# Two of eight weight slots of the first token pair in the seven-product form, with their operand sums early in that pair

## The chip, the cores and the metric

The kernel runs on one core of one Trainium2 chip. The metric is the device time of one execution in microseconds (us), as the median of several runs. The engines named below are TensorE (PE, with PEld for its weight loads), VectorE (DVE), ScalarE (ACT), GpSimd (POOL) and SyncE (SP), which issues most of the DMAs.

## What is computed

The reference is a chunked attention with eight memory tokens, followed by two feed-forward blocks, all in float32:

```python
x = attention(q, k, v, mem_k, mem_v)          # 3072 tokens x 512
h = x @ w_in                                  # 512 -> 2048, the "input product"
g = h * tanh(where(h > 20, h, log1p(exp(min(h, 20)))))
x = g @ w_out                                 # 2048 -> 512
xn = x / sqrt(mean(x * x) + 1e-6) * rms_g
gate, val = xn @ w_gate, xn @ w_val           # 512 -> 1536 each
out = (gate / (1 + exp(-gate)) * val) @ w_out2
```

The weights arrive as 64-bit floats and are converted on the chip. Each float32 operand is held as a rounded part (hi) and a rest (lo), and a product of two operands is three matmuls: hi by hi, hi by lo, lo by hi.

## The kernel before

The change lies in the input product. Its 3072 tokens are eight blocks of 384, taken as four pairs of blocks, and its 2048 output rows are eight weight slots i of 256 rows. The attention of the pair that comes next runs between the matmuls of the pair at hand, so the kernel goes through four stages: attention of pair 0, then the product of pair j beside the attention of pair j + 1.

There are two forms of the product. In the plain form, `unit(b, i)` multiplies slot i with one block b: two output halves, two halves of the 512 inputs, each a `product` of six matmuls (two 128-row pieces by three), so 24 matmuls, and 48 for both blocks of a pair. Its results leave PSUM by one ACT copy per output half (L691). In the seven-product form, `group1(j, i)` treats a slot and a pair of blocks as 2x2 block matrices and needs seven products of six matmuls, 42 in all. It wants sums of blocks as operands: on the weight side `finish(("i", i))` makes them out of a plain converted slot (four DVE additions of 512 and 256 columns, two on POOL, two splits into hi and lo), on the token side `sum_pieces` makes them out of the two blocks `xb` (four DVE operations, L615 to L618, and splits into tiles T). A split is an ACT copy (hi, L153) and a DVE subtraction (lo, L154). Its results leave PSUM by three ACT copies, four DVE operations and one on POOL.

Before the change, pair 0 is plain in all eight slots. Slots 0 to 2 of block 0 are done among the last steps of the attention of pair 0 (`heads`); the other 13 units run in the list `units`, at lines 1045 to 1052: block 1 with slots 0, 1, 2, then both blocks with 3, 4, 7, 5, 6. Pairs 1 to 3 are all in the seven-product form, with the slots in the order 7 to 0 for pair 1.

What stands between the matmuls is set by `slots`: its function `between` is called after each product of six matmuls, and does the next piece of attention, the next step of the weight conversion (`cv_upto`, as a line through a first and a last count), what stands in the table `more` for this count, and over the last seven counts the operand sums of the next pair (`tail_of`). A scheduler then orders each engine's instructions by its own simulation; each engine runs its own list in that order, and an instruction that waits holds up all behind it on its engine.

The tiles T come from a pool of eight buffers (`tp`); pair 0 uses four of them, one for each half of each block, made by `x_split`. The temporary sums and the results share the five buffers named g. In the rows below bk_82 to bk_85 are the PSUM banks of the products, bk_86 and bk_87 those of transposes, and bkp that of the attention's small matmuls (L457 for scores, L506 for values). L393, L436, L489 and L532 are transposes of k, q, the probabilities and the result; L470 and L471 are the maximum and the subtraction of it, L476 the exponential, L539 the copy of an attention result into xb, L202 to L216 the conversion of weights.

## Time and profile before

| what | value |
|---|---|
| median of three runs | 1168.31 us (1165.23 to 1170.05) |
| span of the profiled execution | 1167.0 us |
| PE busy | 1142.3 us, 98% of the span |
| DVE, ACT, POOL busy | 824.7 (71%), 628.7 (54%), 183.3 us (16%) |
| granted TensorE clock, mean | 0.994 |

The span runs from the first to the last instruction; of the profiled execution the page gives no time beside it, and the median of the runs lies 1.31 us above it. The 13 units of pair 0 that the change touches lie at about 66 to 144 us; the product of pair 1 follows. From 65 us on, PE's idle time before any instruction is rarely over 0.4 us. The clock is given as a share of 2.4 GHz.

### The profile page before, as it was taken

The page shows a single profiled execution, that of the slowest core. Times are in us where ns is not written, and L with a number is a line of the kernel's source. Part 1 is how long each engine was busy: PE and PEld are TensorE (multiplying, and loading weights), DVE is VectorE, ACT ScalarE, POOL GpSimd, SP SyncE. Part 2 cuts the span into 40 slices and gives each one's busy share as a digit, 9 for nine tenths or more (in the row PEclk, how much of TensorE's full clock was granted, in tenths as well). Part 3 has the DMA queues.
Part 4 walks back from the last instruction along what each step waited for, and adds up shares of the span by engine and source line. Part 5 has one row for each costly group of instructions (what it writes and reads, how often), then busy time and mean ns, then how long its engine had stood idle before and what let it go on. Part 6 is the DMA issues. An engine that isn't in the chain of part 4 may idle for free.

```text
span 1167.0 us, 22953 instructions
## 1 busy us (share of the span) xinstructions
PE 1142.3 (98%) x9052; PEld 1007.0 (86%) x9052; DVE 824.7 (71%) x1254; ACT 628.7 (54%) x1008; POOL 183.3 (16%) x165
## 2 busy tenths in 40 slices
PE   6899999999999999999999999999999999999998
PEld 4789999999999888888878778888888888999998
DVE  3555798844746876766786765967896857888883
ACT  4566666543555887667775543544454433444441
POOL 3011222310132321010011121110211111000000
PEclk9799999999999999999999999999999999999999
DMA  9889699899488764594599398999899879655421
GB/s 197 171 228 224 183 303 258 230 307 290 151 300 295 257 217 161 172 378 152 199 362 408 126 345 325 349 410 355 316 361 371 316 276 332 191 148 146 145 90 37
DMA packets 213276, 294.20 MB, mean 252 GB/s; under 512 B 104240, under 2 KB 160560, under 8 KB 204336
## 3 DMA queue, kind: packets, MB, share of 16 engines
q1 hardware_dynamic: 210864, 284.34, 73.6%
q0 software_dynamic: 2304, 8.39, 2.3%
q8 instruction: 71, 1.16, 0.4%
q14 instruction: 37, 0.30, 0.1%
HBM read 181.80 MB, written 110.89 MB: 251 GB/s over the span
## 4 chain that ended last, share of the span: by engine, by line
PE 83%; DVE 7%; DMA 5%; ACT 3%; issue 2%; SPq 0%; POOL 0%; ACTq 0%; DVEq 0%
PE bk L639 14%; PE bk L640 13%; PE bk L641 13%; PE bk L914 4%; PE bk L913 4%; PE bk L912 4%; PE bk L755 4%; PE bk L756 4%; PE bk L754 4%; PE bkp L639 2%; PE bkp L641 2%; PE bkp L640 2%; PE bkp L506 1%; PE bkp L457 1%; PE bkp L755 1%
## 5 line engine op out<-in xcount | busy, mean ns | idle before, releaser
L639 PE MATMUL bk<-T,w 128*128 128x384 f32 (+1 forms) x860 | 315.2, 370 | 0.7 <-ACT c L657 0.7
L640 PE MATMUL bk<-T,w 128*128 128x384 f32 (+1 forms) x860 | 311.3, 362 | 0.0
L641 PE MATMUL bk<-T,w 128*128 128x384 f32 (+1 forms) x860 | 308.3, 362 | 0.0
L639 PEld LDWEIGHTS bk<-T,w 128*128 128x128 f32 x860 | 162.3, 189 | 19.9 <-ACT c L657 1.0
L640 PEld LDWEIGHTS bk<-T,w 128*128 128x128 f32 x860 | 162.2, 189 | 16.5 <-DVE T L154 0.3
L641 PEld LDWEIGHTS bk<-T,w 128*128 128x128 f32 x860 | 161.8, 188 | 15.7
L913 PE MATMUL bk<-w,T 128*128 128x256 f32 x396 | 111.9, 283 | 0.0
L914 PE MATMUL bk<-w,T 128*128 128x256 f32 x396 | 111.9, 283 | 0.0
L912 PE MATMUL bk<-w,T 128*128 128x256 f32 x396 | 111.9, 283 | 0.0
L755 PE MATMUL bk<-T,w 128*128 128x512 f32 x276 | 107.5, 390 | 0.2 <-DVE T L154 0.2
L756 PE MATMUL bk<-T,w 128*128 128x512 f32 x276 | 107.1, 389 | 0.0
L754 PE MATMUL bk<-T,w 128*128 128x512 f32 x276 | 105.8, 389 | 0.0
L669 POOL TENSOR_TENSOR v<-c,v 128x512 f32<-128x512 f32 x36 | 54.7, 1519 | 289.2 <-DVE c L665 238.8
L665 DVE TENSOR_TENSOR c<-bk,c 128x512 f32<-128x512 f32 (+2 forms) x72 | 43.0, 597 | 51.2 <-PE bk L641 38.6
L912 PEld LDWEIGHTS bk<-w,T 128*128 128x128 f32 x396 | 76.0, 192 | 0.1
L913 PEld LDWEIGHTS bk<-w,T 128*128 128x128 f32 x396 | 76.0, 192 | 0.1
L914 PEld LDWEIGHTS bk<-w,T 128*128 128x128 f32 x396 | 76.0, 192 | 0.0
L649 ACT COPY c<-bk 128x512 f32<-128x512 f32 (+2 forms) x72 | 37.1, 516 | 69.6 <-POOL v L669 24.7
L154 DVE TENSOR_TENSOR T<-s,T 128x1024 fp32r<-128x1024 f32 (+1 forms) x50 | 63.1, 1269 | 14.3 <-ACT T L153 14.2
L782 ACT ACTIVATE s<-s 128x1024 f32<-128x1024 f32 x44 | 46.4, 1060 | 29.7 <-DMA s<-g_scratch 29.5
L755 PEld LDWEIGHTS bk<-T,w 128*128 128x128 f32 x276 | 51.8, 188 | 11.3 <-DVE T L154 0.6
L754 PEld LDWEIGHTS bk<-T,w 128*128 128x128 f32 x276 | 51.8, 188 | 10.8
(228 smaller groups left out, 2287.1 us busy)
## 6 DMA issues: line engine op xcount, KB each, us to landing
T<-nt_scratch SPq DMA_DIRECT2D x35, 1024.0 KB
g_scratch<-g SPq DMA_DIRECT2D x64, 384.0 KB
s<-g_scratch SPq DMA_DIRECT2D x46, 512.0 KB
h_scratch<-s SPq DMA_DIRECT2D x36, 512.0 KB
w<-wg SPq DMA_DIRECT2D x10, 1792.0 KB
wg<-w SPq DMA_DIRECT2D x30, 512.0 KB
raw<-in_moe_w_out_dram SPq DMA_DIRECT2D x28, 512.0 KB
nt_scratch<-T SPq DMA_DIRECT2D x14, 1024.0 KB
```

The lines of the kernel that those rows point to most:

```text
L154: keep((eng or nc.vector).tensor_tensor(lo, src, hi.bitcast(F32), op=ALU.subtract))
L639: nc.tensor.matmul(ps, whi, xh, start=first and kk == 0, stop=False, **more)
L640: nc.tensor.matmul(ps, whi, xl, start=False, stop=False, **more)
L641: nc.tensor.matmul(ps, wlo, xh, start=False, stop=kk == 1, **more)
L669: nc.gpsimd.tensor_tensor(c22, u3, z5, op=ALU.add)
L754: nc.tensor.matmul(ps, ahi, bhi, start=start, stop=False)
L755: nc.tensor.matmul(ps, ahi, blo, start=False, stop=False)
L756: nc.tensor.matmul(ps, alo, bhi, start=False, stop=stop)
L782: nc.scalar.activation(x, g, self.act)
L912: nc.tensor.matmul(ps, t[:, 0, f], w[:, 0], start=first and f == 0, stop=False, **more)
L913: nc.tensor.matmul(ps, t[:, 0, f], w[:, 1], start=False, stop=False, **more)
L914: nc.tensor.matmul(ps, t[:, 1, f], w[:, 0], start=False, stop=f == HG - 1, **more)
```

## The change

Slots 4 and 7 of pair 0 move to the seven-product form, and the order of the slots becomes: block 1 with 0, 1, 2; both blocks with 3; groups 4 and 7; both blocks with 5 and 6 ("the last two plain"). The token sums of pair 0 are made in the first five counts of the stage (`first_sums`), out of the blocks in place, into the four T buffers that pair 0 had left free (`T_FIRST` takes all eight at once); products 1, 2 and 3 use the T tiles that `x_split` made. `finish` of slots 4 and 7 stands three counts ahead of their groups; that of slot 4 was in the stage of pair 1 before. The weight conversion line is steeper (80 steps over 50 counts, where it was 73 over 52).

```diff
+    T_FIRST = [t_new() for _ in range(8)]
+    X_AT = {(0, 0): 4, (0, 1): 5, (1, 0): 6, (1, 1): 7}
+    P_AT = {6: 0, 5: 1, 4: 2, 7: 3}
     def x_split(b, half):
-        t = t_new()
+        t = T_FIRST[X_AT[b, half]]
...
-    units = [(1, i) for i in range(NHEAD)]
-    units += [(b, i) for i in (3, 4, 7, 5, 6) for b in range(2)]
-    at = {u: 4 * n + 4 for n, u in enumerate(units)}
+    units = [(1, i) for i in range(NHEAD)] + [(b, 3) for b in range(2)]
+    whole = (4, 7)
+    after = [(b, i) for i in (5, 6) for b in range(2)]
+
+    def first_sums():
+        b11, b21, b12, b22 = (xb[b][:, 2 * half:2 * half + 2, :] for b in range(2) for half in range(2))
+        early, rest = sum_pieces(0, b11, b21, b12, b22, lambda: T_FIRST[P_AT[first_p.pop(0)]],
+                                 lambda p: g_new(), None, ttab_x)
+        return [early[1]] + rest[0:3] + rest[4:5]
+
+    first_p = [6, 5, 4, 7]
     more = {}
-    finish_at(more, 7, at[1, 7] + 1)
-    bt = slots((att_list(1), 4 * len(units)), (0, 73), tail_of(1), calls(more), CV_I)
+    for n, call in enumerate(first_sums()):
+        then(more, n + 1, call)
+    for p, bh in ((1, (0, 0)), (2, (0, 1)), (3, (1, 1))):
+        ttab_x[0, p] = xtab[bh]
+    n_slots = 4 * len(units + after) + 7 * len(whole)
+    for n, i in enumerate(whole):
+        finish_at(more, i, 4 * len(units) + 7 * n - 3)
+    bt = slots((att_list(1), n_slots), (0, 80), tail_of(1), calls(more), CV_I)
     for b, i in units:
         run([unit(b, i)], bt)
+    for i in whole:
+        group1(0, i, bt)
+    for b, i in after:
+        run([unit(b, i)], bt)
...
-    for n, i in enumerate((6, 5, 4, 3)):
-        finish_at(more, i, 3 * n + 1)
+    for n, i in enumerate((6, 5, 3)):
+        finish_at(more, i, 4 * n + 1)
```

What this does to the order shows at three places. The first is ACT's list at the start of the pair, where the second block of the pair is finished and split. L406 and L407 copy transposed keys, L153 with w is the hi part of slot 2's second half, L153 with T that of block 1. Before:

```order
L407 COPY kw<-bk_86 128x4x32
L539 COPY xb<-bk_87 128x4x128
L153 CAST w<-ca 128x2x2x128
L153 CAST T<-xb 128x768 x2
L447 COPY qT<-bk_87 128x512
L406 COPY kw<-bk_86 128x4x3x56
L407 COPY kw<-bk_86 128x4x32
L202 ACTIVATE ca<-raw 128x512
L205 ACTIVATE lr<-raw 128x512
```

The same stretch of ACT's list after the change:

```order
L407 COPY kw<-bk_86 128x4x32
L202 ACTIVATE ca<-raw 128x512
L205 ACTIVATE lr<-raw 128x512
L539 COPY xb<-bk_87 128x4x128
L153 CAST w<-ca 128x2x2x128
L406 COPY kw<-bk_86 128x4x3x56
L407 COPY kw<-bk_86 128x4x32
L153 CAST T<-xb 128x768 x2
```

The two conversion steps L202 and L205 of the next weight half now stand ahead of the last copy into xb and of the slot's cast.

The second place is DVE's list at the same time, from the last parts of the block's split to the next maximum of the attention. Before:

```order
L410 COPY kw<-kw 128x16x8
L154 TENSOR_TENSOR w<-ca,w 128x2x2x128
L402 COPY kw<-bk_86 128x4x24
L154 TENSOR_TENSOR T<-xb,T 128x768 x2
L470 TENSOR_REDUCE mx<-bkp 128x8
```

The same stretch of DVE's list after the change:

```order
L210 SCALAR_TENSOR_TENSOR ca<-raw,ca 128x512
L615 TENSOR_TENSOR xb<-xb 128x768
L154 TENSOR_TENSOR w<-ca,w 128x2x2x128
L154 TENSOR_TENSOR T<-xb,T 128x768 x2
L616 TENSOR_TENSOR g<-xb 128x768
L618 TENSOR_TENSOR xb<-xb 128x768
L617 TENSOR_TENSOR g<-g,xb 128x768
L154 TENSOR_TENSOR T<-g,T 128x768
L154 TENSOR_TENSOR T<-xb,T 128x768
L154 TENSOR_TENSOR T<-g,T 128x768
L154 TENSOR_TENSOR T<-xb,T 128x768
L470 TENSOR_REDUCE mx<-bkp 128x8
```

A conversion step and the first sum now stand ahead of the lo part of slot 2's second half, and eight operations of 768 columns in all are new there.

The third place is PE's list at the end of the pair, from the last matmuls of the last unit to the first product of pair 1. The rows with bk_85 belong to the unit, those with bk_82 to pair 1. Before, the last transpose L532 of the attention of pair 1 stands 24 matmuls ahead of the unit's end, and the list ends with:

```order
L639 MATMUL bk_85<-T,w 128x384
L640 MATMUL bk_85<-T,w 128x384
L641 MATMUL bk_85<-T,w 128x384
L393 MATMUL bk_87<-ident,kn 128x128
L436 MATMUL bk_86<-ident,qn 128x128 x4
L393 MATMUL bk_87<-ident,kn 128x128 x3
L639 MATMUL bk_82<-T,w 128x384
```

The end of PE's list of pair 0 after the change:

```order
L532 MATMUL bk_86<-ident,x 128x128 x4
L641 MATMUL bk_85<-T,w 128x384
L639 MATMUL bk_85<-T,w 128x384
L640 MATMUL bk_85<-T,w 128x384
L641 MATMUL bk_85<-T,w 128x384
L393 MATMUL bk_87<-ident,kn 128x128 x4
L436 MATMUL bk_86<-ident,qn 128x128 x8
L393 MATMUL bk_87<-ident,kn 128x128 x4
L457 MATMUL bkp<-kw,qT 32x64 x3
L639 MATMUL bk_82<-T,w 128x384
```

L532 now stands four matmuls ahead of the unit's end, and the transposes of two query tiles follow one another in the same bank.

## Rows read from the trace of the kernel before

**Rows 1.** The page, first part: busy time, share of the span, instructions.
```profile
PE 1142.3 (98%) x9052; PEld 1007.0 (86%) x9052; DVE 824.7 (71%) x1254; ACT 628.7 (54%) x1008; POOL 183.3 (16%) x165
```

**Rows 2.** Stretches of 30 us: busy time of each engine, clock, DMA share, GB/s.
```profile
60.00:90.00 30.00, 29.13 (x402) 27.32 (x384) 17.00 (x34) 19.46 (x39) 6.27 (x8) 1.00 0.85 217
...
150.00:180.00 30.00, 30.00 (x424) 28.07 (x424) 29.17 (x56) 18.87 (x39) 9.23 (x11) 1.00 0.99 298
...
240.00:270.00 30.00, 30.00 (x497) 27.72 (x490) 12.10 (x25) 12.39 (x25) 2.19 (x3) 1.00 0.94 305
```

**Rows 3.** Timeline of PE: start us, us, instruction; first and last of 17 in succession.
```profile
74.90 0.33 PE L639 MATMUL bk<-T,w 128*128 128x384 f32 x1
...
77.68 0.33 PE L640 MATMUL bk<-T,w 128*128 128x384 f32 x1
```

**Rows 4.** Timeline of ACT at the start of pair 0, idle time before in brackets.
```profile
63.37 0.60 ACT L539 COPY xb<-bk 128x512 f32<-128x512 f32 x1
63.84 0.64 ACT L153 CAST w<-ca 128x512 fp32r<-128x512 f32 x1
64.36 1.59 ACT L153 CAST T<-xb 128x768 fp32r<-128x768 f32 x2
...
67.08 0.73 ACT L202 ACTIVATE ca<-raw 128x512 f32<-128x512 f32 x1
67.66 0.72 ACT L205 ACTIVATE lr<-raw 128x512 int32<-128x512 uint32 x1
```

**Rows 5.** Timeline of DVE at the start of pair 0.
```profile
64.52 1.00 DVE L154 TENSOR_TENSOR w<-ca,w 128x512 fp32r<-128x512 f32 x1 [0.41 <-ACT w L153]
65.44 0.24 DVE L402 COPY kw<-bk 128x96 f32<-128x96 f32 x1
65.61 2.29 DVE L154 TENSOR_TENSOR T<-xb,T 128x768 fp32r<-128x768 f32 x2
...
74.75 0.68 DVE L210 SCALAR_TENSOR_TENSOR ca<-raw,ca 128x512 int32<-128x512 int32 x1
```

**Rows 6.** Timeline of PE at the start of pair 0.
```profile
63.86 0.66 PE L393 MATMUL bk<-ident,kn 128*128 128x128 f32 x4 [0.87 <-DVE kw L410]
64.36 0.60 PE L436 MATMUL bk<-ident,qn 128*128 128x128 f32 x4
64.71 0.42 PE L639 MATMUL bk<-T,w 128*128 128x384 f32 x1
...
65.84 0.33 PE L641 MATMUL bk<-T,w 128*128 128x384 f32 x1
```

**Rows 7.** Timeline of DVE at the start of pair 1: first two sums, first split.
```profile
140.37 0.96 DVE L615 TENSOR_TENSOR xb<-xb 128x768 f32<-128x768 f32 x1
141.36 0.96 DVE L616 TENSOR_TENSOR g<-xb 128x768 f32<-128x768 f32 x1
...
143.98 1.59 DVE L154 TENSOR_TENSOR T<-g,T 128x768 fp32r<-128x768 f32 x1
```

**Rows 8.** Timeline of PE there: the attention's last transpose, second matmul of product 6.
```profile
138.76 0.60 PE L532 MATMUL bk<-ident,x 128*128 128x128 f32 x4
...
145.62 0.44 PE L640 MATMUL bk<-T,w 128*128 128x384 f32 x1
```

**Rows 9.** Stretches, PE alone: busy, clock, DMA share, GB/s; the first two bound six.
```profile
43.00:44.00 1.00, 0.97 (x51) 0.50 0.54 92
...
48.00:49.00 1.00, 1.00 (x4) 0.50 1.35 168
...
600.00:610.00 10.00, 8.80 (x39) 1.00 1.04 408
```

**Rows 10.** Timeline of PE: a wait ahead of that stretch at half clock, in brackets.
```profile
42.80 1.53 PE L506 MATMUL bkp<-vw,pT 64*32 64x65 f32 x52 [1.40 <-DMA vw<-in_v_dram]
```

**Rows 11.** Timeline of DVE: first and last operations of the finish of slot 7.
```profile
122.16 0.68 DVE L290 TENSOR_TENSOR ca<-w 128x512 f32<-128x512 f32 x1
...
129.02 1.29 DVE L154 TENSOR_TENSOR w<-sm,w 128x768 fp32r<-128x768 f32 x2
```

## The prediction

> **What bounds the kernel now.** I read the page's busy times first. PE works 1142.3 us of a span of 1167.0 [rows 1], so a change is worth what it does to PE's list: work taken out of it, less waits put into it. Then I read the stretches by time. In the product of pair 0 PE is busy for 29.13 of 30 us at the start and all the time later, at clock 1.00 [rows 2]. DVE is the next engine: 17.00 of 30 us at the start of the pair, but 29.17 of 30 at 150 to 180 us, in the stage of pair 1 [rows 2]; PE hardly waits even there. Last I read the timelines of PE, ACT and DVE at the two ends of pair 0, where the order of the new program differs most from the old. There the reader is to look for how late an operand is ready before PE takes it: at both ends the old program has almost nothing to spare.
>
> **What is taken out.** Two slots go from 48 matmuls to 42, so 12 matmuls of 384 columns leave PE's list. One of them is recorded with 0.33 us, but they overlap: 17 in succession start between 74.90 and 77.68 us, 2.78 us for 16 steps, 0.174 us each [rows 3]. The gain is 12 x 0.174 = 2.1 us, which is 0.18% of the time, and not the 4 us that the recorded durations would suggest. No DMA is added or taken away; the results are stored in as many bytes as before. That caps the whole change: only waits that vanish could add to it, and PE has almost none in these stages.
>
> **What is added beside PE.** For the token sums DVE gets four operations of 0.96 us [rows 7] and four lo parts of the same size, some 7.7 us; ACT gets four hi parts of about 0.8 us (two took 1.59) [rows 4]. The groups' results cost eight DVE operations, two POOL operations and two ACT copies less. The finish of slot 4 comes over from the next stage, which DVE's load at 150 to 180 us [rows 2] can only welcome. None of it is on PE, and DVE has 13 us of 30 free at the start of the pair [rows 2]. So I cost it at nothing, except where an instruction now stands ahead of one that PE is waiting for. That is so at two places.
>
> **First place, the start of the pair.** In ACT's list L202 and L205 now precede the copy L539 and the cast of slot 2's second half. Before, they came at 67.08 and 67.66, 0.58 us for the first and about as much for the second [rows 4]; together 1.15 us. Before, L539 started at 63.37 and the cast ended near 64.5 [rows 4], and PE took up the transpose L436 at 64.36 and the first matmul on that cast at 64.71 [rows 6]: it had 0.2 us to spare. So ACT's 1.15 us come through as about 1.1 us of waiting on PE. Next comes the lo part of the same weights. Before, it was done at 65.5 [rows 5], and PE wanted it at 65.84 [rows 6]. Now DVE's list has L402, L210 and L615 first. L615 needs the late L539 (ready at about 65.2 with the delay), takes 0.96 us [rows 7], and then the lo part takes 0.7: ready at about 67.0. PE, itself 1.1 us late and without the two matmuls that stood between, wants it at about 66.5. That is another 0.5 us. The splits of block 1 follow with PE 1.3 us of other matmuls behind, and are in time. First wait: 1.6 us, with 0.5 (the conversion's data land later or ACT is ahead of this row) and 2.5 (both delays in full) as ends. The long DVE block behind it, up to L470, holds up the attention's maximum to about 76 us; PE reaches what depends on it only some 33 matmuls and eight transposes after the scores, about 79 us by the same walk, so it is hidden; without that cover each operation left over would cost 0.96 us.
>
> **Second place, the end of the pair.** The operands of pair 1 depend on the last attention tile: L532, copy, L615, L616, hi, lo. Before, L532 started at 138.76 and the second matmul of product 6, which needs the first lo part, at 145.62 [rows 8], right behind that lo part (143.98 plus 1.59) [rows 7]. So the chain takes 6.8 us, and PE filled it with 24 matmuls, eight transposes and the first product: the wait was near nothing. Now only four matmuls stand behind L532. PE has these (0.7 us and a start of 0.3), 16 transposes (some 1.8), the first product (1.0 and a start) and a few small ones, 4.5 to 5 us of work. The copy no longer queues behind L406 and L407, which shortens the chain to about 6.4. PE loses the difference, 1.4 to 1.9 us, first at the second query tile, which waits until ACT has emptied the bank of the first, then at the keys behind DVE's L410. I take 1.65, with 0.5 (DVE and ACT free earlier) and 3 (a conversion step in between) as ends. Nothing else is late next: the later splits follow every 0.95 us, a product takes 1.04.
>
> **Between the two** the groups need their weight sums. The finish of slot 7 took from 122.16 to 130.3 us, 8.1 us among other work [rows 11]; its bare chain is near 5. The order puts the matmuls that need the lo parts behind products 4 and 2, so product 6 of group 4 has about 5 us for the hi parts and 7.8 for the lo parts. I cost this at nothing, with 2 us for each group as the upper end.
>
> **The sum:** -2.1 + 1.6 + 1.65 = +1.2 us (rounded up from 1.15). Against the span, 1168.2; the median lies 1.31 us above the span, so I say 1169.5 us. Ends: -2.1 + 0.5 + 0.5 = -1.1, and -2.1 + 2.5 + 3 + 4 = +7.4.
>
> **A rule against the change.** The seven-product form goes round four PSUM banks, one product after another, and waits for evictions of three engines. At 240 to 270 us, where the kernel does nothing but this form beside attention, the granted clock is 1.00 [rows 2], the level of 2.4 GHz. The Trainium skill, TensorE: Matmul & The Clock Gate, section "A second HAM failure mode: psum-queue depth-cycling", says that a kernel that cycles through PSUM banks can idle TensorE briefly and often enough that its clock swings between the half and the full rate. By that rule the sum would be up to +15.8, by the row it is +1.2, and the trace does not agree with the rule here. As a mechanism of this kernel: the 84 matmuls of the two groups take 84 x 0.174 = 14.6 us at the full rate and up to 29.2 at the half rate, which would give up to 1184.1.
>
> **Rivals.**
> *The waits are covered* (the scheduler's order turns out well): the 2.1 us arrive whole, 1166.2. For it: PE's waits from 65 us on are tiny before [rows 2], although the lists there also look tight. Against it: both slacks were used up before, 0.2 us and nothing [rows 6, 8].
> *The half clock, the case on the slow side.* Before 42.80 PE waited 1.40 us, and then ran six whole microseconds at 0.50 [rows 9, 10], 1.2 GHz; ten microseconds with 1.2 us of waiting at 600 us [rows 9] and the stretch around the wait of 0.87 at 63.86 [rows 2, 6] stayed at 1.00. Six microseconds at half rate do three microseconds of work, so one fall costs 3.0 to 3.5. If both new waits come as one piece and reach 1.40 us, where this trace shows a fall, both stretches are slow: 1169.5 + 6.5 = 1176.0, slower by 0.7%; with one fall it is 1172.7. Against it: the early stretch was full of other waits, and both new waits are split into two pieces of 0.5 to 1.2 us between dense matmuls. The Trainium skill, same page, section "HAM oscillation — how this bites in real kernels", says that idle gaps between bursts bring the half rate back and that each return is paid; no row shows gaps of the new size amid dense work.
> *Late weight sums*: the finish of slots 4 and 7 runs as long as it did for slot 7 and DVE, fuller now, does it last: 1 to 2 us for each group, 1171.5 to 1173.5.
> *The change not doing what it says* is excluded by the order: PE's list is 12 matmuls shorter.
>
> **How the numbers follow.** Forecast (both waits, no fall) 0.52; covered 0.24; late weight sums 0.12; half clock after the waits 0.08; bank cycling at the half clock 0.01; anything else 0.03. A measurement of this kernel can tell about 0.5%, 5.8 us, from no change. Below 1162.5 no case reaches, except the unnamed rest: faster 0.03. Above 1174.2 lie the bank cycling, the half clock with both falls, and the worst of the late sums with large waits: slower 0.07. Same 0.90. The range takes in the forecast and the covered case with the spread of the runs, and the late sums: 1165.0 to 1174.0.
>
> **What would show it.** Right: 12 matmuls fewer; PE idle of about 1 us before L436 or the first L639 behind it near 64 us and half a microsecond before an L641; about 1.2 us before the second query tile's L436 and 0.6 before L393 at the end of the pair; middle stages unchanged. Wrong: PE idle inside groups 4 and 7, a clock under 1.00 near 70 or 145 us, or a difference that arises behind 330 us, where the lists are the same up to about 1000 us.

## The result, and the profile after

The changed kernel takes 1178.19 us (median of six, 1175.75 to 1180.56) against 1168.36 (six, 1165.23 to 1170.05): a ratio of 1.0081, interval 1.0065 to 1.0097. It is slower by 9.8 us. The prediction said 1169.5 with 1174.0 as its upper end, so both the time and the range were wrong. The profiled execution has a span of 1174.7 us, 7.7 more than that of before. It is one of the two fastest of the six, so its profile accounts for 7.7 of the 9.8 us; what makes the others longer it can't show.

The first part of the page after, which answers to [rows 1]: busy time, share, instructions.

```profile
PE 1142.9 (97%) x9040; PEld 1004.7 (86%) x9040; DVE 836.2 (71%) x1270; ACT 630.8 (54%) x1010; POOL 188.9 (16%) x167
```

The 12 matmuls are gone (9052 to 9040), yet PE's busy time has not fallen, so it is no measure of the change. To place the 7.7 us I compare starts of instructions that both programs have:

| stretch | before | after | difference |
|---|---|---|---|
| start to the last attention tile of pair 0 (13th L532) | 51.99 | 51.49 | -0.5 |
| from there to the first matmul of the w_out product (L754, after: L758) | 271.18 | 277.24 | +6.1 |
| first to last matmul on that line | 311.83 | 315.41 | +3.6 |
| from there to the first of the last product (L912, after: L916) | 344.76 | 343.74 | -1.0 |
| the rest of the span | 187.24 | 186.82 | -0.4 |

So there are two losses: one in the input product, where the change is, and one some 400 us behind the matmuls that were taken out, in a product whose instructions stand in the same order in both programs. These are PE's waits of the first, from the timeline of PE after (start, duration, instruction, idle time ahead of it and what ended it); of before, only the old waits at L393 [rows 6] and at an L489 of pair 1 (0.36 us) are over 0.3 us there.

```profile
64.66 0.66 PE L436 MATMUL bk<-ident,qn 128*128 128x128 f32 x4 [0.63 <-ACT xb L539]
66.93 0.45 PE L641 MATMUL bk<-T,w 128*128 128x384 f32 x1 [0.77 <-DVE w L154]
114.82 0.45 PE L639 MATMUL bk<-T,w 128*128 128x384 f32 x1 [0.45 <-ACT w L153]
120.14 0.66 PE L489 MATMUL bk<-ident,p 128*128 128x128 f32 x4 [0.66 <-ACT p L476]
146.13 0.66 PE L436 MATMUL bk<-ident,qn 128*128 128x128 f32 x4 [1.03 <-ACT qT L447]
147.78 0.66 PE L393 MATMUL bk<-ident,kn 128*128 128x128 f32 x4 [0.99 <-DVE kw L410]
183.55 0.44 PE L639 MATMUL bk<-T,w 128*128 128x384 f32 x1 [0.66 <-DVE c L665]
```

The first two and the fifth and sixth are the waits predicted, at the instructions predicted. The other three are new. The stretches say who took DVE's room (busy time of PE, PEld, DVE, ACT, POOL, then the clock, DMA share and GB/s):

```profile
60.00:90.00 30.00, 27.73 (x345) 25.05 (x343) 24.34 (x41) 21.88 (x43) 7.44 (x8) 1.00 0.85 211
100.00:125.00 25.00, 23.86 (x390) 21.86 (x395) 23.75 (x47) 17.24 (x33) 5.93 (x9) 1.00 0.87 219
140.00:150.00 10.00, 7.98 (x56) 7.17 (x55) 5.72 (x9) 5.28 (x11) 2.39 (x2) 1.00 0.81 225
```

DVE went from 17.00 of 30 us [rows 2] to 24.34, and is busy for 23.75 of the 25 us at the groups, where it was 14.89 before. The clock is 1.00 in all three. The same 25 us before:

```profile
100.00:125.00 25.00, 25.00 (x450) 23.02 (x448) 14.89 (x29) 16.32 (x31) 2.89 (x4) 1.00 0.93 233
```

The second loss, timeline of PE after in the w_out product:

```profile
535.73 1.20 PE L758 MATMUL bk<-T,w 128*128 128x512 f32 x4 [0.84 <-ACT T L153]
570.80 0.49 PE L837 MATMUL bk<-v,ones_r 128*128 128x512 f32 x1 [2.23 <-ACT v L153]
```

Both waits hang on ACT, and ACT hangs on a load of results of the input product. This is ACT after, and then the same instruction before (there L782):

```profile
525.24 1.06 ACT L786 ACTIVATE s<-s 128x1024 f32<-128x1024 f32 x1 [6.93 <-DMA s<-g_scratch]
```
```profile
516.77 1.06 ACT L782 ACTIVATE s<-s 128x1024 f32<-128x1024 f32 x1 [5.43 <-DMA s<-g_scratch]
```

Measured from the first matmul of the product, ACT goes on at 196.5 us after and at 193.6 before.

### The profile page after: what moved, and what is told of

Read it like the earlier page. It is cut to its first block, busy times and chain, and to the rows that moved or that the text cites. A ratio compares the mean times of both kernels' runs of the same rounds, so it can differ in the third digit from the quotient of the medians.

```text
span 1174.7 us, 22965 instructions
## 1 busy us (share of the span) xinstructions
PE 1142.9 (97%) x9040; PEld 1004.7 (86%) x9040; DVE 836.2 (71%) x1270; ACT 630.8 (54%) x1010; POOL 188.9 (16%) x167
## 3 DMA queue, kind: packets, MB, share of 16 engines
q8 instruction: 71, 1.16, 0.4%
## 4 chain that ended last, share of the span: by engine, by line
PE 79%; DVE 7%; DMA 7%; ACT 4%; issue 2%; SPq 0%; POOL 0%; ACTq 0%; DVEq 0%
PE bk L639 14%; PE bk L641 13%; PE bk L640 13%; PE bk L918 4%; PE bk L917 4%; PE bk L916 4%; PE bk L759 3%; PE bk L760 3%; PE bk L758 3%; DMA s<-g_scratch 3%; PE bkp L639 2%; PE bkp L640 2%; PE bkp L641 2%; PE bkp L457 2%; DVE T L154 1%
## 5 line engine op out<-in xcount | busy, mean ns | idle before, releaser
L639 PE MATMUL bk<-T,w 128*128 128x384 f32 (+1 forms) x856 | 314.3, 370 | 2.1 <-DVE c L665 0.9
L641 PE MATMUL bk<-T,w 128*128 128x384 f32 (+1 forms) x856 | 307.3, 361 | 0.8 <-DVE w L154 0.8
L639 PEld LDWEIGHTS bk<-T,w 128*128 128x128 f32 x856 | 161.2, 189 | 22.5 <-DVE c L665 1.3
L641 PEld LDWEIGHTS bk<-T,w 128*128 128x128 f32 x856 | 160.8, 188 | 16.8 <-DVE w L154 1.1
L916 PE MATMUL bk<-w,T 128*128 128x256 f32 x396 | 112.0, 283 | 0.0
L758 PE MATMUL bk<-T,w 128*128 128x512 f32 x276 | 105.9, 390 | 0.8 <-ACT T L153 0.8
L916 PEld LDWEIGHTS bk<-w,T 128*128 128x128 f32 x396 | 76.0, 192 | 0.1
L758 PEld LDWEIGHTS bk<-T,w 128*128 128x128 f32 x276 | 51.7, 188 | 12.0 <-ACT T L153 1.3
```

The costliest lines, as they stand in the source:

```text
L639: nc.tensor.matmul(ps, whi, xh, start=first and kk == 0, stop=False, **more)
L641: nc.tensor.matmul(ps, wlo, xh, start=False, stop=kk == 1, **more)
L758: nc.tensor.matmul(ps, ahi, bhi, start=start, stop=False)
L916: nc.tensor.matmul(ps, t[:, 0, f], w[:, 0], start=first and f == 0, stop=False, **more)
```

## The experiments

All kernels in one table; the diffs below it show the main lines of each edit. "Pairs" is the second row of the table above and "w_out" the third. "Transfer" is where, counted from the first matmul of the w_out product, a transfer of TensorE's own instructions begins (rounded down to 0.5 us; more on it at e10), and "ACT" the wait for the load of results that follows it. The times of before in the four sets of runs were 1169.17, 1167.00, 1169.21 and 1169.69 us. Each row rests on one profile, and the row e5 is the kernel before against itself: it came out at 1.0017, with an interval that leaves out 1, so differences of about 0.2% between ratios say nothing.

| kernel | median us | ratio and interval | pairs | w_out | transfer | ACT |
|---|---|---|---|---|---|---|
| before | 1168.36 | - | 271.18 | 311.83 | 170.5 | 5.43 |
| after | 1178.19 | 1.0081 (1.0065 to 1.0097) | 277.24 | 315.41 | 175.5 | 6.93 |
| e1 after again | 1176.76 | 1.0077 (1.0047 to 1.0108) | 282.92 | 314.71 | 174.5 | 7.52 |
| e2 late conversion | 1175.84 | 1.0066 (1.0041 to 1.0090) | 279.37 | 316.26 | 174.0 | 6.13 |
| e3 attention early | 1174.84 | 1.0060 (1.0040 to 1.0080) | 276.05 | 315.56 | 176.5 | 7.26 |
| e4 late conversion and sums | 1172.57 | 1.0037 (1.0020 to 1.0054) | 274.17 | 315.17 | 176.0 | 6.45 |
| e5 before again | 1169.25 | 1.0017 (1.0001 to 1.0033) | 270.90 | 311.96 | 170.5 | 4.51 |
| e6 early finish | 1175.48 | 1.0067 (1.0047 to 1.0087) | 278.48 | 315.99 | 175.5 | 7.45 |
| e7 no sums, no groups | 1174.19 | 1.0069 (1.0045 to 1.0093) | 275.99 | 311.59 | 170.0 | 5.22 |
| e8 sums, no groups | 1176.36 | 1.0090 (1.0056 to 1.0124) | 277.51 | 311.73 | 171.0 | 4.41 |
| e9 before, line to 80 | 1172.89 | 1.0039 (1.0022 to 1.0056) | 276.66 | 311.11 | 170.5 | 5.29 |
| e10 split stores | 1173.06 | 1.0039 (1.0024 to 1.0054) | 274.35 | 315.97 | 175.5 | 6.51 |
| e11 one group | 1181.83 | 1.0110 (1.0076 to 1.0145) | 278.76 | 315.59 | 174.5 | 7.20 |
| e12 list lengthened | 1176.07 | 1.0048 (1.0031 to 1.0065) | 276.52 | 312.39 | 171.0 | 5.71 |
| e13 list shortened | 1169.38 | 0.9998 (0.9983 to 1.0014) | 270.83 | 315.20 | 175.0 | 6.37 |

### First set: the two ends of the pair

**e1** is the changed kernel as it is.

> The changed kernel once more, for a second look at where its time is lost. In the first look PE was 5.56 us behind the kernel before at the end of the input product (first L754 at 328.73 against 323.17 us), and lost 3.6 us more between 530 and 571 us, in the product with w_out, where it waits for tiles loaded from g_scratch. Theory A, the new waits in pair 0 are fixed by the order and the 3.6 us belong to the DMAs of that one execution: 5.4 to 5.7 us behind again at the end of the input product, and the loss at 500 to 600 us lies anywhere between 0 and 4. Theory B, the later loss follows from the change: 3 to 4 us again at the same two places. Median 1176 to 1180 us either way.

Its pairs took 282.92 us, 5.7 more than in the first profile. The waits of the first profile are there again, the one at L641 longer, and two more: 0.80 us at an L457 at 103.35 and 1.32 at the L639 behind it, for a hi part from ACT. The larger part of the 5.7 us is the clock: first the wait behind which it begins to fall, then stretches of PE with the granted clock in the column behind the count.

```profile
66.04 0.51 PE L641 MATMUL bk<-T,w 128*128 128x384 f32 x1 [1.41 <-DVE w L154]
```
```profile
66.00:68.00 2.00, 1.96 (x7) 0.57 1.24 178
68.00:70.00 2.00, 2.00 (x9) 0.58 1.09 252
150.00:152.00 2.00, 1.28 (x11) 0.90 0.82 187
152.00:154.00 2.00, 2.00 (x8) 0.50 1.16 365
```

Twice the clock fell towards 0.50, the level of 1.2 GHz, once behind the waits at the start of the pair and once behind those at its end. Two us at 0.57 and two at 0.58 cost 1.7 us of work, the second fall about 1.6 (0.1 of 1.28, half of 2.00 and a quarter of the 2 us behind, at 0.75). That is 3.3 of the 5.7 us; the further waits make up the rest. In the first profile the same two places stayed at 1.00. So the half clock after a wait is real in this kernel, but not certain: it comes in some executions and not in others.

**e2** starts the conversion of pair 0 two counts later.

```diff
-    bt = slots((att_list(1), n_slots), (0, 80), tail_of(1), calls(more), CV_I)
+    bt = slots((att_list(1), n_slots), (2, 82), tail_of(1), calls(more), CV_I)
```

> The weight conversion of pair 0 starts two counts later and as steep, nothing else; ACT's list then has L539 and the cast of slot 2 ahead of L202 and L205, as in the kernel before, and the last L532 of the pair stays one matmul from its end. Theory A (each wait has its own cause in the order): the 0.63 us before L436 and the 0.77 us before L641 near 65 us are gone or under 0.3 together, the two waits of about 1.0 us at the end of the pair stay, the end of the input product comes about 1.4 us earlier than with the change (4.1 us behind the kernel before). Rival (DVE is simply too full, a wait removed comes back further on): 5 us or more behind at the end of the input product.

Timeline of PE: the wait at L436 at the start is gone, the one for the lo part stays, and new ones appear.

```profile
67.15 0.44 PE L641 MATMUL bk<-T,w 128*128 128x384 f32 x1 [0.86 <-DVE w L154]
117.95 0.86 PE L506 MATMUL bkp<-vw,pT 64*32 64x65 f32 x64 [0.92 <-DVE p L471]
148.59 0.66 PE L393 MATMUL bk<-ident,kn 128*128 128x128 f32 x4 [1.16 <-DVE kw L410]
```

L202 and L205 ahead of the copy did cause the first wait. The second belongs to the first token sum (L615), which still stands ahead of the lo part on DVE. The clock fell to 0.50 at 152 us, so the pairs' 279.37 us are no measure of the waits alone. Less some 1.7 us for the fall they are still 6.5 us over before, as the rival expected, and not 4.1.

**e3** lets the attention of the next pair end four counts earlier.

```diff
-            span = n_slots - 7
+            span = n_slots - att_end     # 7 by default, 11 for pair 0
```

> The attention pieces of pair 0's stage are spread over four counts less, nothing else; the last L532 then stands 16 matmuls ahead of the pair's end instead of 4. Theory A: the two waits of about 1.0 us before L436 and L393 at the end of the pair are gone or under 0.4 together, those near 65 us stay at 0.6 and 0.8; about 2.0 us less, 3.6 us behind the kernel before at the end of the input product. Rival (the token sums are late whatever stands before them): the waits stay at 1.5 to 2 us together, on the lo parts of T.

Timeline of PE at the end of the pair: L436 and L393 no longer wait, but the first products of pair 1 do.

```profile
147.27 0.44 PE L639 MATMUL bk<-T,w 128*128 128x384 f32 x1 [0.78 <-ACT g L695]
149.27 0.44 PE L640 MATMUL bk<-T,w 128*128 128x384 f32 x1 [0.45 <-DVE T L154]
```

The 2.0 us at the end became 1.2, and attention pressed into fewer counts waits elsewhere (0.86 us at an L506 at 116.88). In the pairs 1.2 us were gained, not the 2.0 expected: the wait moved more than it went.

**e4** has the late conversion of e2 and makes the token sums five counts later.

```diff
-        then(more, n + 1, call)
+        then(more, n + 6, call)
```

> The conversion starts two counts later and the token sums of pair 0 five counts later; by the order the first place is as before the change, and the last L532 stands 18 matmuls ahead of the pair's end. Theory A: all four waits gone, only those at group 7 (0.45 and 0.66 us in the changed kernel) may stay: 0 to 2.5 us behind the kernel before at the end of the input product, median 1168 to 1173 us. Theory B adds 3.6 us in the product with w_out as long as the two groups are there: 1172 to 1176. Rival (DVE too full): 4 us or more behind at the end of the input product.

All four predicted waits are gone, at both ends, up to 0.26 us at the L641. What is left in the pair, timeline of PE:

```profile
103.74 0.44 PE L639 MATMUL bk<-T,w 128*128 128x384 f32 x1 [1.38 <-ACT w L153]
114.10 0.44 PE L639 MATMUL bk<-T,w 128*128 128x384 f32 x1 [0.97 <-ACT w L153]
119.88 0.45 PE L639 MATMUL bk<-T,w 128*128 128x384 f32 x1 [0.75 <-ACT w L153]
```

These are the weight sums of slots 4 and 7: PE waits for their hi parts for 3.1 us, beside 0.47 us at an L506. With both ends mended the kernel is 0.37% slower than before, where the change as it is loses 0.81%.

### Second set: what the groups have to do with it

**e5** is the kernel before, profiled again.

> The kernel before, unchanged, profiled a second time. The question is the product with w_out, at 500 to 620 us, where all five profiles with the change lose 1.2 to 3.7 us against the one profile of the kernel before (252.3 us from the first to the 300th L754, against 253.5 to 256.0), though no instruction there differs. Theory A (the change delays the loads and results there): the second profile again has 252.0 to 252.7 us and no wait at L837 for ACT v L153 over 1 us. Theory B (it is chance from one execution to the next, and the first profile was a lucky one): the second has 253.5 us or more with such a wait. Clock 1.00 from 50 us on by either. Time 1165 to 1171 us.

The w_out product took 311.96 us, as in the first profile (311.83), and the clock stayed at 1.00 from 50 us to the last two. So the second loss is the change's doing and no chance.

**e6** takes e4 and makes the weight sums two counts earlier, with a steeper conversion to feed them.

```diff
-        finish_at(more, i, 4 * len(units) + 7 * n - 3)
+        finish_at(more, i, 4 * len(units) + 7 * n - 5)
-    bt = slots((att_list(1), n_slots), (2, 82), tail_of(1), calls(more), CV_I)
+    bt = slots((att_list(1), n_slots), (2, 104), tail_of(1), calls(more), CV_I)
```

> Late conversion and late token sums as in e4, and the weight sums of slots 4 and 7 two counts earlier, with the conversion line steeper (104 steps where it was 82) so that the slots are ready for it. In e4 PE waited 1.38 us at group 4 and 0.97 + 0.75 us at group 7 for the hi part of the weight sums. Theory A (these late weight sums are what is left of the loss): the three waits fall under 0.4 us, the pair ends 2 to 2.5 us earlier than in e4, and the time is 1169.5 to 1171. Theory B (DVE is simply full at 100 to 122 us, so that what comes earlier there pushes something else late): other waits of 0.4 to 1 us come at L506 or L489 behind the maximum and the exponential, and the time stays at 1172 to 1174.

Timeline of PE: no wait for a hi part is left, and others have come.

```profile
111.50 0.44 PE L639 MATMUL bk<-T,w 128*128 128x384 f32 x1 [2.06 <-ACT c L649]
125.03 0.86 PE L457 MATMUL bkp<-kw,qT 64*32 64x64 f32 x64 [1.09 <-DVE x L522]
146.24 0.66 PE L436 MATMUL bk<-ident,qn 128*128 128x128 f32 x4 [1.03 <-ACT qT L447]
```

Waits of 2.06 + 1.09 us stand where e4 has 1.38 + 0.97 + 0.75, under other names; the steeper line also brought the wait at the end of the pair back. Theory B fits in kind: between 100 and 125 us DVE is full, and what is moved ahead there pushes something else behind. But the edit changes two things at once and doesn't tell which of them brought the 2.06 us, and the time, 1175.48, is above what either theory gave. Its pairs also hold a wait of 1.16 us for a load of v at 58.89 us, ahead of the places of the edit.

**e7** makes slots 4 and 7 plain again and drops the token sums. What stays of the change is the order of the ends, the steeper line, and a finish of slot 4 in pair 0.

```diff
-        group1(0, i, bt)
+        for b in range(2):
+            run([unit(b, i)], bt)
```

> The changed kernel with slots 4 and 7 plain again, so that there are no token sums, no groups, and the matmuls are as many as before the change; the steeper conversion line, the slot order and the order at both ends of the pair stay as changed (L202 and L205 ahead of the last copy into xb; L532 four matmuls ahead of the unit's end). The weight sums of 4 and 7 are made later in the pair. Theory A (the waits at both ends come from the steeper conversion and the way attention is spread, not from the groups): PE waits about 0.6 us at L436 near 64 us, none at L641 for DVE, and 1.0 + 1.0 us at L436 and L393 at the pair's end; the time is 1170.5 to 1172.5. Theory B (the groups and their sums cause nearly all of the loss): the waits at the ends are under 0.5 us together, and the time is 1168 to 1169.5.

Timeline of PE:

```profile
64.89 0.66 PE L436 MATMUL bk<-ident,qn 128*128 128x128 f32 x4 [0.62 <-ACT xb L539]
145.78 0.66 PE L436 MATMUL bk<-ident,qn 128*128 128x128 f32 x4 [1.03 <-ACT qT L447]
147.08 0.66 PE L393 MATMUL bk<-ident,kn 128*128 128x128 f32 x4 [0.65 <-DVE kw L410]
```

Without a single group or token sum, three of the four predicted waits are there, and the kernel is 0.69% slower than before (1174.19 us, above the 1172.5 of theory A). The wait at L641 is gone, so that one is the token sums' own. The rows also show that a wait costs more than its bracket: from the L393 ahead to this L436 it is 1.27 us (63.62 to 64.89), where the kernel before needs 0.50 [rows 6], so a wait of 0.62 delays by 0.77; at the end, 1.03 delays by about 1.2.

**e8** is e7 with the token sums made early and used by nothing.

> As e7, but the token sums of pair 0 are made early in the pair as in the change, and nothing uses them: eight operations of about 0.96 us more on DVE and four casts on ACT, with all slots plain. Theory A (the token sums cost PE only the wait for the lo part of slot 2's second half): PE waits about 0.8 us more at an L641 near 67 us than in e7 and nowhere else over 0.4 us; the time is 0.7 to 1.2 us above e7. Theory B (the block of DVE work delays the attention's maximum and exponential, and the half clock follows): further waits at L506 or L489 at 75 to 90 us and a granted clock under 0.9 at 64 to 72 us; 2 to 4 us above e7.

The wait for the lo part comes back, and no other does; the clock stays at 1.00 there. Timeline of PE:

```profile
68.21 0.44 PE L641 MATMUL bk<-T,w 128*128 128x384 f32 x1 [0.95 <-DVE w L154]
```

The pairs take 1.5 us more than in e7; by the medians it is 2.2 us, more than the 1.2 of theory A, with overlapping intervals. The block of DVE work hid as predicted, except for the one place at its head.

### Third set: one number, the stores, one group

**e9** is the kernel before with one number changed.

```diff
-    bt = slots((att_list(1), 4 * len(units)), (0, 73), tail_of(1), calls(more), CV_I)
+    bt = slots((att_list(1), 4 * len(units)), (0, 80), tail_of(1), calls(more), CV_I)
```

> The kernel before with one number changed: the conversion line of pair 0 ends at 80 where it ended at 73. No token sums, no groups, no other slot order. The order of both ends of the pair then is that of the changed kernel: L202 and L205 ahead of the last copy into xb, the last L532 three matmuls ahead of the unit's end with two query tiles behind one another. Theory A (that number alone makes most of the loss, and the seven-product form is nearly innocent): waits of about 0.6 us at L436 near 65 us and of 1.0 and 0.7 to 1.0 us at L436 and L393 at the pair's end, 4 to 5 us more than before from the stage's start to the first L754, and a time of 1172 to 1175, a ratio of 1.004 to 1.007. Theory B (e7's loss came from the weight sums of slot 4 that it makes in pair 0): 1168 to 1170.

Timeline of PE, and the stretch behind the two waits at the end:

```profile
64.41 0.66 PE L436 MATMUL bk<-ident,qn 128*128 128x128 f32 x4 [0.61 <-ACT xb L539]
145.27 0.66 PE L436 MATMUL bk<-ident,qn 128*128 128x128 f32 x4 [1.03 <-ACT qT L447]
146.56 0.72 PE L393 MATMUL bk<-ident,kn 128*128 128x128 f32 x4 [0.64 <-DVE kw L410]
```
```profile
148.00:150.00 2.00, 2.00 (x8) 0.50 1.03 430
```

The end point of the conversion's line, 80 instead of 73, reorders both ends of the pair by itself: some of the conversion's steps come a count sooner, the scheduler puts two of them ahead of the last copy into xb, and the last attention tile moves from 24 matmuls ahead of the unit's end to three. This one number makes 0.39% of loss, about half of the change's. Its pairs, 276.66 us, hold one fall of the clock and a wait of 1.01 us in pair 1, at an L639 at 178.03 for DVE.

**e10** is e4 with the groups' results of pair 0 stored block by block, in the row length of the plain form.

```diff
+            if j == 0:
+                for a in range(2):
+                    store_later(g_d[2 * i + e, :, a * N:a * N + N], g[e][:, a, :])
+                continue
```

> e4 (late conversion, late token sums) with the results of the two groups stored block by block, in rows of 1536 bytes as the plain form stores them, not in rows of 3072; all else as in e4. The six profiles with groups in pair 0 took 253.5 to 256.2 us from the first to the 300th L754, the four without 251.9 to 252.9, with the same orders there and the same bytes; only the stores of pair 0 differ (512 packets fewer with groups). Theory A (the way these stores are cut sets how the loads of the w_out product share the queues): 252 to 252.9 us, and 1 to 1.5 us less than e4 in all. Theory B (the stores have nothing to do with it): 253.5 us or more, and e4's time, 1171 to 1174.

Nothing changed in the w_out product: 315.97 us, the first 300 steps 256.95. Theory A fell. Timeline of PE there (L841 is L837 of the other kernels) and the stretch that begins behind the wait:

```profile
567.64 0.59 PE L841 MATMUL bk<-v,ones_r 128*128 128x512 f32 x1 [1.79 <-ACT v L153]
```
```profile
568.00:570.00 2.00, 2.00 (x6) 0.50 0.56 156
```

The clock can fall behind this wait as well. Since neither the order, nor the bytes, nor the cut of the stores set the kernels with groups apart, I looked at the transfers that the profile lists as instructions. There are 71 on one queue, 1.16 MB, so 16 KB each. The Trainium skill, Trainium Architecture — The Big Picture, section "The software stack", gives 64 bytes for an instruction; 9040 matmuls and as many weight loads then make an estimated 1.16 MB, which agrees with this queue being TensorE's list. In this trace the transfers come all through the run. 9040 matmuls on 71 transfers are one for about 127 matmuls with their loads, so each should come at a fixed place of the list. The one in the table does: it begins behind 5411 to 5422 matmuls, counted from the start of the program, in all 15 profiles. With 12 matmuls fewer in pair 0 it comes at least 12 matmuls of the w_out product later, and the column "transfer" shows it, at 170 to 171 us without groups and at 174 to 176.5 with them.

**e11** keeps only slot 7 as a group and puts slot 5 ahead of it, so that all sums have ten counts more.

```diff
-    units = [(1, i) for i in range(NHEAD)] + [(b, 3) for b in range(2)]
-    whole = (4, 7)
-    after = [(b, i) for i in (5, 6) for b in range(2)]
+    units = [(1, i) for i in range(NHEAD)] + [(b, i) for i in (3, 4, 5) for b in range(2)]
+    whole = (7,)
+    after = [(b, 6) for b in range(2)]
```

> Only slot 7 in the seven-product form, slot 4 plain; slot 5 is converted and multiplied ahead of it, so that the weight sums and the token sums of the group have ten counts more before they are wanted; conversion from the third count on, the attention's steps ended two counts earlier. The groups' gain is then half, 6 x 0.174 = 1.0 us. Theory A (all that was lost in the pair were waits for things that came too late, so with time for them the gain arrives): no PE wait over 0.4 us from 65 to 150 us, 270 to 271 us from the stage's start to the first L754, and a time of 1167.5 to 1169.5. Theory B (eight more DVE operations and the sums cost PE something wherever they stand): waits of 0.5 to 1.5 us at L506 or L489 or for the lo parts, and 1171 to 1174.

The slowest of all. Timeline of PE:

```profile
113.06 0.44 PE L639 MATMUL bk<-T,w 128*128 128x384 f32 x1 [1.58 <-ACT w L153]
137.12 0.44 PE L639 MATMUL bk<-T,w 128*128 128x384 f32 x1 [0.94 <-DVE c L654]
151.52 0.44 PE L639 MATMUL bk<-T,w 128*128 128x384 f32 x1 [0.94 <-ACT g L695]
```

The first is a plain slot's converted weights, late because other slots were converted ahead; the clock fell to 0.52 behind it. The others are results that wait for DVE and ACT at the end of the pair, beside the sums of pair 1. The kernel also has a confounder that I had overlooked: the groups' PSUM banks go by a count of groups, and one group instead of two or none shifts all later groups by four banks, so its 5 us more behind the w_out product say nothing on pair 0. It does not tell whether groups can be had without waits.

### Fourth set: the length of TensorE's list

**e12** is e4 with 12 transposes done twice, later on, so that the list in front of the w_out product is as long as before.

```diff
-        for a in range(NP):
+        for a in list(range(NP)) * (2 if t in (12, 13, 14) else 1):
```

> e4 (late conversion, late token sums) with 12 transposes done twice, in the stage of pair 1 (L532 of three query tiles, into the same bank, the same result), so that TensorE's list is as long in front of the w_out product as it was before the change. In the traces the transfers that bring TensorE's own instructions come at fixed places of its list: from 170 to 174 and 198 to 202 us behind the first matmul of the w_out product in the five profiles without groups, from 174 to 178 and 202 to 206 us in the seven with groups that were read so; and the same split parts 251.9 to 252.9 us from 253.5 to 256.2 us for the first 300 steps of that product. Theory A (12 matmuls fewer in pair 0 move these transfers into the stretch where the loads of results are already late, and PE pays 1 to 4 us for it): the transfers come at 170 to 174 us again, the 300 steps take 252 to 253 us, no wait at L837 for ACT v L153 over 0.5 us, and the time is that of e4 or a little less (1171 to 1172.5) in spite of 1.3 us of transposes done twice. Theory B (something else of the groups does it): 253.5 us or more, and 1173 to 1175.

**e13** is the kernel before without 12 matmuls (the two with a lo part in six products of pair 0; those terms are missing from its output).

```diff
-            nc.tensor.matmul(ps, whi, xl, start=False, stop=False, **more)
-            nc.tensor.matmul(ps, wlo, xh, start=False, stop=kk == 1, **more)
+            short and kk == 0 or nc.tensor.matmul(ps, whi, xl, start=False, stop=False, **more)
+            short and kk == 0 or nc.tensor.matmul(ps, wlo, xh, start=False, stop=kk == 1, **more)
```

> The kernel before with 12 matmuls left out of the plain product of pair 0 (in six products of slots 3 and 4, the two with a lo part of the first input half; these terms are missing in its output). No groups, no sums, the order at both ends as before; only TensorE's list is 12 matmuls shorter, as with the change. Theory A (the length of the list alone shifts the instruction transfers): they come at 174 to 178 and 202 to 206 us behind the first matmul of the w_out product, the 300 steps take 253.5 us or more, with waits at L837 for ACT v L153 and at L759; of the 2.1 us taken out nothing is left at the end, 1167 to 1170. Theory B (the list's length has no part in it): 252 to 252.9 us, and the 2.1 us arrive, 1165.5 to 1167.5.

Timeline of ACT, its wait for the load of results, in e12 and then in e13, and timeline of PE of e13, its waits:

```profile
523.63 1.06 ACT L786 ACTIVATE s<-s 128x1024 f32<-128x1024 f32 x1 [5.71 <-DMA s<-g_scratch]
```
```profile
518.36 1.06 ACT L782 ACTIVATE s<-s 128x1024 f32<-128x1024 f32 x1 [6.37 <-DMA s<-g_scratch]
```
```profile
131.64 0.66 PE L532 MATMUL bk<-ident,x 128*128 128x128 f32 x4 [0.74 <-DVE x L522]
145.25 0.44 PE L640 MATMUL bk<-T,w 128*128 128x384 f32 x1 [0.63 <-DVE T L154]
563.75 0.67 PE L833 MATMUL bk<-v,ones_r 128*128 128x512 f32 x1 [2.04 <-ACT v L153]
```

Groups with the old length: transfer at 171.0, w_out in 312.39 us, no wait at L837 for ACT v. No groups with the shorter length: transfer at 175.0, w_out in 315.20, the wait there. Both of these products fit theory A and neither fits theory B: the length of the list does it, not the groups. Over all 15 profiles the two kinds do not overlap: 311.11 to 312.39 us where the transfer comes before 172 us, 314.71 to 316.26 where it comes at 174.0 or later, and ACT's wait 4.41 to 5.71 against 6.13 to 7.52.

What the transfer meets at the one place and at the other shows in the stretches around it, in before (the first) and after (the second): DMA share and GB/s are the last two columns.

```profile
493.20:495.20 2.00, 2.00 (x10) 1.00 0.03 8
```
```profile
503.70:505.70 2.00, 2.00 (x10) 1.00 1.06 420
```

Early it has the engines to itself. Late it falls into a burst of stores at 420 GB/s. There ACT begins to fall behind, in steps: it waits for stores of nt_scratch to land, then for the load of results. In the kernel after it has two waits for stores there, in the kernel before one:

```profile
504.79 2.00 ACT L153 CAST T<-T 128x1024 fp32r<-128x1024 f32 x2 [3.34 <-DMA nt_scratch<-T]
...
509.73 1.05 ACT L153 CAST T<-s 128x1024 fp32r<-128x1024 f32 x1 [0.56 <-DMA nt_scratch<-T]
```
```profile
498.50 2.01 ACT L153 CAST T<-T 128x1024 fp32r<-128x1024 f32 x2 [2.71 <-DMA nt_scratch<-T]
```

Measured from the first matmul of the product, ACT is 0.1 us later than in the kernel before until the first of these waits, 0.7 us later after it, 1.4 after the second and 2.9 after the wait for the load. The second wait (0.51 to 1.22 us) is there in seven of the nine profiles with a late transfer and in none with an early one; in the other two, e2 and e11, the first is longer (4.70 and 4.69). One transfer is 12.0% of sixteen engines for half a microsecond, about 0.96 us of one engine. This is the DMA view of after for the half microsecond from 504.23 us (queue, packets, MB, share of 16 engines):

```profile
q8 instruction: 1, 0.02, 12.0%
```

The Trainium skill, DMA: Bandwidth & Descriptors, section "Queues, rings and completion order", says that a DMA engine takes turns between its queues and drains a whole packet of one before it goes to the next. The rows agree with a delay by a packet of another queue. That this packet is what delays the stores is argued from the place and not shown by itself, and why 1 us on one engine becomes 2 to 3 us at ACT no run shows.

The total of e12 missed its expectation by 3.6 us, and was above theory B's range too. In its profile the w_out product gave back 2.8 us against e4; the transposes and a wait of 0.73 us at an L489 cost 2.4, the 1.0 us that the shifted kernels get back behind that product was lost again, and a wait of 1.33 us at 888 us for a load of nt_scratch came, which e3 and e9 also have (1.98 and 0.94) and the other kernels have not. That wait is not explained. And e13 did not fall below before because 1.4 us of its 2.1 turned into waits in pair 0 already (the first two rows), and the w_out product lost more than what was left. So the loss in the w_out product is shown in the profiles, but what it is worth in the whole time is not: by the medians e12, which doesn't have it, is not faster than e4, which has it, and e13, which has it, is no slower than before (-2.0 to +1.6 us).

## Why the prediction was wrong, point by point

The step that failed is the sum: it had waits at two places of pair 0 and put everything else at nothing. These two came nearly as forecast, but the input product took 6.1 us more in the profile after, where -2.1 + 1.6 + 1.65 had been counted: further waits in both pairs, a start behind every wait, and 1.7 us that stay open. The w_out product and what follows it took another 2.6, for which there was no term.

**Right: the arithmetic of what is taken out.** 12 matmuls fewer. But the step that counted them as gain, "-2.1", holds only if nothing else in the pair is as tight as PE. e13 takes out 12 matmuls and adds nothing, and its pairs take 270.83 us against 271.18 and 270.90: 0.1 to 0.4 us arrive. The slack that I had read in DVE's busy share is not there at the end of the pair, where PE waits for the operands of pair 1.

**Right: both places, the instructions, and nearly the sizes.** Predicted 1.6 and 1.65 us; shown 0.63 + 0.77 = 1.40 and 1.03 + 0.99 = 2.02, plus about 0.2 us a wait for the start behind it, which I had not counted. e7 and e9 make clear what I told only half: three of the four come from the end point of the conversion's line and need no group. Only the wait for the lo part is the token sums'.

**Wrong: "Between the two" at nothing.** The weight sums and the attention at the groups cost 0.45 + 0.66 us in the profile after, and 3.1 us for hi parts alone in e4. The finish of slot 7 again takes as long as in [rows 11]:

```profile
109.50 1.29 DVE L290 TENSOR_TENSOR ca<-w 128x512 f32<-128x512 f32 x2
...
116.80 0.41 DVE L154 TENSOR_TENSOR w<-sm,w 128x256 fp32r<-128x256 f32 x1
```

That is 7.7 us, where I had counted on "near 5" for a bare chain. I had this rival, with a chance of 0.12 and 1 to 2 us a group; it came in full in e4 and in part in the profile after, because the finish cannot begin before its slot is converted, and the conversion is only just ahead of PE: in e4 the lo part that ends slot 4's conversion starts at 98.71 us on DVE, the finish at 99.44, and PE waits for its result from 102.4 to 103.74. Pair 1 adds 0.66 us for group results behind a full DVE. "Nothing else is late next" had looked at the splits alone.

**Wrong: "middle stages unchanged".** I had taken the same order for the same time, and even named a difference behind 330 us as a sign of error. The w_out product lost 3.6 us and 1.0 came back later, 2.6 in all, in the profile; e12 and e13 put it down to the length of TensorE's list. No term of the sum stood for it, and no rival.

**The half clock: the rival was right in kind and wrong in price and chance.** I gave it 0.08, and 3.0 to 3.5 us a fall, from the six microseconds of [rows 9]. It fell in e1 twice, and once in e2, e3, e9, e10, e11 and e13, each time behind one wait of 1.58 to 2.04 us or two in short succession (the smallest 1.03 + 0.64), with 1.6 to 1.7 us lost by each of the two in e1. It did not fall in the profile after, behind the same pairs of waits and one of 2.23 us. Neither before nor e5 fell once between 50 us and the last two. The Trainium skill, TensorE: Matmul & The Clock Gate, section "HAM oscillation — how this bites in real kernels", says that idle gaps between bursts of matmuls bring the half rate back; the rows of e1 and e9 agree, those of after and e7 show that waits of this size need not do it, and I had set that rule aside because no row of before had gaps of this size.

**Bank cycling** did not happen: at the groups the clock is 1.00 (100 to 125 us, above).

**The balance.** PE's new waits in the pairs sum to 5.5 us (those shown and one of 0.29 in pair 1), less the old 0.36; with 0.2 us for each of the seven more starts and less 2.1 for the matmuls that is some 4.4 of the 6.1 us lost there. The other 1.7 us I can't assign: they are not idle time of PE, whose other gaps there add only 0.2 us. By the medians, e9 (the order of the ends alone) loses 0.39% and e4 (the ends mended, the groups kept) 0.37%; together 0.76%, close to the change's 0.81%; with 0.2% of noise between ratios this says no more than about half each. e7 lost more than e9 in its runs, with overlapping intervals.

**The range.** The sum of all upper ends was +7.4 us, 1175.7 by the median, and the profiled execution, 1176.45, was above it. I had cut the range at 1174.0 because each mishap had a small chance of its own. I take it that they were not independent: one full engine, DVE, stood ahead of the lo part, the hi parts, the exponential and the results of pair 1. That is argued from its busy share; no run frees DVE alone.

None of the kernels with a group is faster than before, and what they could gain at best, 2.1 us or 0.18%, is less than these runs can tell. Of all that was run, the kernel before stays the one to use.

## What to carry to other kernels

When PE is 98% busy, work taken out of its list is a gain only where the next engine's chains have slack at that very place; read the slack from the timelines of the operands, not from a busy share over 30 us. A pacing constant is part of a change: run it alone first, since here 73 to 80 alone made about half of the loss. And an order that is the same is not a time that is the same: look where the transfers of the instruction lists fall before calling later stages unchanged.

## What the hardware showed that I had not expected

- The transfers of TensorE's own instructions (71 of 16 KB) take part in the traffic. Twelve matmuls more or fewer, placed 300 to 400 us ahead, move one of them by 3 to 6 us, from a stretch at 8 GB/s into one at 420 or back, and with it a product takes 315 to 316 us in place of 312.
- The clock falls to 0.50 behind a wait of 1.58 to 2.04 us, or two close together, amid dense matmuls, in some executions and not in others, at the same place of the same program (after and e1), and the visible price is 1.6 to 1.7 us.
- A PE wait delays the list by 0.15 to 0.2 us more than the idle time shown at it (0.62 shown, 0.77 lost).
